# Casting and transposing one operand in two pieces, with two idle matmuls fewer ahead of the first scores

## Chip, cores, metric

One core of one Trainium2 chip. The metric is the device time of one execution, in microseconds (us). Executions of one and the same program scatter here by about 0.4 us (standard deviation), so a change of half a microsecond needs many runs, and single profiles are read for where the time goes, not for how much there is of it. "ScalarE" is the engine that the profile calls ACT, "VectorE" is DVE, "GpSimd" is POOL and "TensorE" is PE.

## The reference

Chunked attention feeds a two-layer network with a swish whose slope is given for each hidden unit. Shapes: q, k, v are 8 x 8 x 576 x 64 in fp32; w_in is 512 x 2048, w_out 2048 x 512.

```python
scores = scale * np.matmul(q_c, k_c.transpose(0, 1, 2, 4, 3))   # chunks of 64
scores = scores - np.max(scores, axis=-1, keepdims=True)
attn = np.exp(scores)
attn = attn / (np.sum(attn, axis=-1, keepdims=True) + 1e-09)
out = np.matmul(attn, v_c)
...
h = x @ w_in
g = h * (1.0 / (1.0 + np.exp(-beta * h)))
return (g @ w_out).astype(np.float32)
```

## The kernel before

After the first 18 us the kernel is a stream of dense matmuls that fills TensorE to the end. The change and the argument are about the opening, where TensorE has no data yet. There it runs "idle" matmuls on zeros, which raise its clock. One of them, called late, waits for a small memset that GpSimd executes between two DMA issues, and so ties the rest to a fixed moment (4.8 us). The first 512 tokens come in two halves of four heads. Heads 0 to 3 come through the sync queue as fp32 (`raw0`) and are cast by ScalarE; heads 4 to 7 come through GpSimd's queue, which casts on the way (`qk0[1]`). VectorE transposes both in blocks of 32 x 32.

```python
    def emit_T_half(a):
        for i in (0, 1):                      # q, then k
            if a == 0:
                nc.scalar.copy(out=qk0[a][i], in_=raw0[i])
            nc.vector.transpose(out=qkT0[a][i]..., in_=qk0[a][i]...)   # cut

    def emit_sc_half(u, a):                   # 4 heads of unit u
        ...                                   # cut
        qt, kt = qkT0[a]
        for h in range(HH):                   # HH = 4
            ...                               # 8 small matmuls a head

    # the opening, in TensorE's order
        emit_tiny(78)
        warm = idle_bank()
        emit_idle(3, 512, warm)
        nc.tensor.matmul(out=warm[:, 0:16], lhsT=idle[:, 0:128], rhs=late)
        emit_idle(10, 512, warm)
        emit_T_half(0)
        emit_sc_half(0, 0)                    # "first scores"
        emit_ex_half(0, 0)
        warm = idle_bank()
        emit_idle(6, 512, warm)
        emit_T_half(1)
        nc.vector.transpose(out=bt, in_=braw)
        emit_sc_half(0, 1)                    # "second scores": heads 4 to 7
        emit_ex_half(0, 1)
        emit_sc_half(1, 0)
        emit_idle(2, 512, warm)
        ...                                   # cut: issues of later loads
        emit_pv(0, ("s", "p"))                # needs v tiles 0 and 1
        ...
```

The softmax here doesn't subtract the row's maximum and nothing guards it: scores larger than these inputs give would overflow.

Of the kernel before, what the change touches and what calls it, by code (L numbers as in the profile page):

```python
# [8 lines left out]
FP32 = mybir.dt.float32  # L9
# [6 lines left out]
def kernel(  # L16
# [10 lines left out]
    nc = tc.nc  # L27
# [31 lines left out]
    HH = H // 2  # L59
    raw0 = [const.tile([128, HH, 4, D], FP32, name=f"raw{i}") for i in range(2)]  # L60
    qk0 = [[const.tile([128, HH, 4, D], FP16, name=f"h0{i}{a}") for i in range(2)] for a in range(2)]
    qkT0 = [[const.tile([128, HH, 128, 2], FP16, name=f"t0{i}{a}") for i in range(2)] for a in range(2)]
# [109 lines left out]
    xt_t = {}  # L172

    def emit_T_half(a):
        for i in (0, 1):
            if a == 0:
                nc.scalar.copy(out=qk0[a][i], in_=raw0[i])
            nc.vector.transpose(
                out=qkT0[a][i].rearrange("p h s e -> p (h s e)").bitcast(FP32).rearrange(
                    "p (h i r) -> p h r i", h=HH, r=4),  # L180
                in_=qk0[a][i].rearrange("p h r d -> p (h r d)").bitcast(FP32).rearrange(
                    "p (h r i) -> p h r i", h=HH, r=4),
            )

    def emit_sc_half(u, a):
# [135 lines left out]
    def emit_m(j, m, c0=0, n=None, later=False):  # L321
        n = blocks[j][1] * UNIT if n is None else n
        if j not in gt_t:
            gt_t[j] = gt_p.tile([128, KFF, 512], FP16, tag="gt", name="gt")
        hps = ps_p.tile([128, 512], FP32, tag="p", name="hps")
        xr = xt_t[j].rearrange("p t (r k) (c q) -> p (t r) (k c) q", r=2, c=2)
        for kk in range(KDM):
            nc.tensor.matmul(  # L328
                out=hps[:, 0:n],
                lhsT=w_in16[m // 2][:, kk, (m % 2) * 128:(m % 2) * 128 + 128],  # L330
                rhs=xr[:, c0 // CH:(c0 + n) // CH, 2 * (kk % 2) + kk // 2, :],
                start=(kk == 0),
                stop=(kk == KDM - 1),
            )
        sg = sg_p.tile([128, 512], FP32, tag="sg", name="sg")

        def act():
            nc.scalar.activation(  # L338
                out=sg[:, 0:n], in_=hps[:, 0:n], func=ACTF.Tanh, scale=beta2[:, m:m + 1])

        def vec():
            nc.vector.scalar_tensor_tensor(  # L342
                out=gt_t[j][:, m, c0:c0 + n], in0=sg[:, 0:n], scalar=1.0, in1=hps[:, 0:n],
                op0=ALU.add, op1=ALU.mult,
            )

        if later:
            return act, vec
        act()
        vec()  # L350
# [23 lines left out]
    def idle_bank():  # L374
        return ps_p.tile([128, 512], FP32, tag="p", name="warm")

    def emit_idle(n, w, d=None):
        d = idle_bank() if d is None else d
        for _ in range(n):
            nc.tensor.matmul(out=d[:, 0:w], lhsT=idle[:, 0:128], rhs=idle[:, 0:w])  # L380
# [12 lines left out]
    with tc.manual_schedule():  # L393
# [4 lines left out]
        for a, eng, dst in ((0, nc.sync, raw0), (1, nc.gpsimd, qk0[1])):  # L398
            for i, src in enumerate((q, k)):
                eng.dma_start(  # L400
                    out=dst[i],
                    in_=src[0, HH * a:HH * a + HH, 0:2 * UNIT, :].rearrange("h (p r) d -> p h r d", r=4),
# [19 lines left out]
        warm = idle_bank()  # L422
        emit_idle(3, 512, warm)
        nc.tensor.matmul(out=warm[:, 0:16], lhsT=idle[:, 0:128], rhs=late)
        emit_idle(10, 512, warm)
        emit_T_half(0)
        emit_sc_half(0, 0)
        emit_ex_half(0, 0)
# [4 lines that stand above are left out]
        emit_sc_half(0, 1)  # L433
# [16 lines left out]
        d = [emit_m(0, m, 0, 256, True) for m in (0, 1)]  # L450
# [145 lines left out]
        for c0, n in ((0, 256), (256, 128), (384, 128)):  # L596
            ops = ps_p.tile([128, DM], FP32, tag="p", name="ops")
            for kk in range(KFF):
                nc.tensor.matmul(  # L599
                    out=ops[:, 0:n],  # L600
# [42 lines left out]
```

## Time and profile before

| | before |
|---|---|
| time, first three runs | 288.23, 288.73, 288.71 us |
| span of the profiled execution | 286.7 us |
| TensorE busy | 98% of the span, 96% of the chain that ended last |
| first scores start | 8.84 us |
| second scores start | 10.62 us |
| w_in products run without a break from | 17.77 us |

Read it from the end backwards. From 17.77 us TensorE has no pause that could be won, so a change in the opening is worth just what it moves that moment. The prediction below shows the chain, the timeline and the page for it. One view is added: the transfers of heads 4 to 7 by the moment of their issue (size, and us from issue to landing). They are issued at 1.24 and 2.12 us.

```profile
h<-in_q_dram POOLq DMA_DIRECT2D x1, 256.0 KB, 6.0
h<-in_k_dram POOLq DMA_DIRECT2D x1, 256.0 KB, 6.6
```

### The profile page before, as it was taken

How to read it: one execution, taken by the hardware profiler on the slowest of the kernel's cores; microseconds unless marked ns; L12 is line 12 of the kernel's file. 1: busy time of each engine (PE TensorE's matmuls, PEld its weight loads, DVE VectorE, ACT ScalarE, POOL GpSimd, SP SyncE). 2: the span in 40 equal slices, each digit the busy share in tenths (PEclk: the TensorE clock that was granted, in tenths of full speed). 3: DMA queues.
4: the chain of work that ended last, by engine and by line, in shares of the span. 5: the costliest groups of instructions: out<-in, count | busy, mean ns of one | idle time of the engine just before them, and what ended most of it. 6: DMA issues, size and time to landing. Idle time of an engine off the chain costs nothing.

```text
span 286.7 us, 6657 instructions
## 1 busy us (share of the span) xinstructions
PE 280.5 (98%) x2779; PEld 136.4 (48%) x2779; DVE 141.8 (49%) x259; ACT 146.9 (51%) x224; POOL 95.7 (33%) x125
## 2 busy tenths in 40 slices
PE   6989999999999999999999999999999999999995
PEld 3564456545544444444444444444444444444444
DVE  2678544776567544534454445454554545333300
ACT  4478228774557545454545454554545444444411
POOL 8853678487172983070907070000000000000000
PEclk9999999999999999999999999999999999999999
DMA  8999999999999999999999999565451212001012
GB/s 197 177 197 206 182 179 212 207 165 164 152 97 179 148 175 162 177 123 162 140 165 105 175 122 174 130 75 128 57 129 37 75 37 75 37 37 39 37 73 75
DMA packets 139997, 37.14 MB, mean 130 GB/s; under 512 B 126912, under 2 KB 135488, under 8 KB 139968
## 3 DMA queue, kind: packets, MB, share of 16 engines
q0 software_dynamic: 99136, 17.83, 81.1%
q1 hardware_dynamic: 40688, 18.83, 32.4%
q8 instruction: 22, 0.36, 0.5%
q10 hardware_dynamic: 144, 0.07, 0.1%
q14 instruction: 7, 0.06, 0.1%
HBM read 36.71 MB, written 9.44 MB: 161 GB/s over the span
## 4 chain that ended last, share of the span: by engine, by line
PE 96%; ACT 1%; POOL 1%; issue 1%; DVE 0%; DVEq 0%; POOLq 0%
PE hps L328 44%; PE ops L360 43%; PE warm L380 2%; PE x L265 2%; PE sc L237 1%; PE sc L224 1%; PE ops L599 1%; ACT xt L303 1%; PE xp L302 1%; POOL h L400 1%; POOL vbig L113 1%; PE sc L197 0%; ACT et L207 0%; PE y L265 0%; PE xp L310 0%
## 5 line engine op out<-in xcount | busy, mean ns | idle before, releaser
L342 DVE SCALAR_TENSOR_TENSOR gt<-sg,hps 128x512 f16<-128x512 f32 (+1 forms) x153 | 99.1, 654 | 107.3 <-ACT sg L338 107.1
L338 ACT ACTIVATE sg<-hps,beta 128x512 f32<-128x512 f32 (+1 forms) x153 | 100.4, 663 | 73.0 <-PE hps L328 72.9
L328 PE MATMUL hps<-xt,win 128*128 128x512 f16 (+1 forms) x612 | 136.9, 367 | 0.8 <-ACT xt L303 0.7
L360 PE MATMUL ops<-wout,gt 128*128 128x512 f16 x560 | 131.2, 379 | 0.0
L328 PEld LDWEIGHTS <-win 128*128 128x128 f16 x612 | 58.1, 98 | 62.1 <-issue 1.0
L360 PEld LDWEIGHTS <-gt 128*128 128x128 f16 x560 | 53.9, 98 | 63.4
L370 ACT ACTIVATE osb<-ops 128x512 f32<-128x512 f32 x35 | 20.9, 598 | 42.5 <-PE ops L360 42.5
L113 POOL DMA_DIRECT2D vbig<-in_v_dram x40 | 34.0, 870 | 10.9 <-DMA wout<-in_moe_w_out_dram 3.7
L99 POOL DMA_DIRECT2D qu<-in_q_dram x22 | 18.7, 864 | 40.6 <-DMA qT<-qu 37.6
L286 DVE TENSOR_TENSOR x<-x,rd 128x512 f16<-128x512 f32 x31 | 21.4, 692 | 1.2
L99 POOL DMA_DIRECT2D ku<-in_k_dram x22 | 18.9, 884 | 0.0
L284 DVE RECIPROCAL rd<-x 128x8 f32<-128x8 f32 x31 | 6.2, 201 | 12.5 <-PE x L265 12.5
L246 ACT ACTIVATE et<-sc 128x1024 f16<-128x1024 f32 (+1 forms) x8 | 6.4, 811 | 8.2 <-PE sc L237 8.2
L230 ACT ACTIVATE et<-sc 128x1024 f16<-128x1024 f32 x10 | 10.2, 1018 | 0.2
L265 PEld LDWEIGHTS <-et 64*64 64x64 f16 x576 | 6.0, 107 | 7.3 <-issue 3.8
L380 PE MATMUL warm<-idle 128*128 128x512 f16 x24 | 8.4, 499 | 0.0
L105 POOL DMA_DIRECT2D ku<-in_k_dram x9 | 6.8, 758 | 2.5 <-DMA win<-in_moe_w_in_dram 1.3
L105 POOL DMA_DIRECT2D qu<-in_q_dram x9 | 6.8, 766 | 2.0 <-DMA win<-in_moe_w_in_dram 1.4
L265 PE MATMUL x<-vbig,et 64*64 64x65 f16 x496 | 7.3, 194 | 0.2 <-ACT et L207 0.2
L611 DVE TENSOR_SCALAR osb<-ops 128x256 f32<-128x256 f32 (+1 forms) x2 | 0.7, 358 | 12.1 <-PE ops L599 12.1
L131 POOL DMA_DIRECT2D win<-in_moe_w_in_dram x8 | 6.0, 764 | 1.2 <-DMA vbig<-in_v_dram 1.2
L303 ACT COPY xt<-xp 128x512 f16<-128x512 f16 x9 | 5.1, 588 | 2.3 <-PE xp L302 2.2
(46 smaller groups left out, 73.0 us busy)
## 6 DMA issues: line engine op xcount, KB each, us to landing
out_dram<-osb SPq DMA_DIRECT2D x35, 256.0 KB, 4.0
vbig<-in_v_dram POOLq DMA_DIRECT2D x32, 128.0 KB, 7.8
qu<-in_q_dram POOLq DMA_DIRECT2D x20, 128.0 KB, 5.4
ku<-in_k_dram POOLq DMA_DIRECT2D x20, 128.0 KB, 7.3
win<-in_moe_w_in_dram POOLq DMA_DIRECT2D x8, 256.0 KB, 8.8
wout<-in_moe_w_out_dram POOLq DMA_DIRECT2D x4, 512.0 KB, 12.2
qu<-in_q_dram POOLq DMA_DIRECT2D x3, 256.0 KB, 7.4
ku<-in_k_dram POOLq DMA_DIRECT2D x3, 256.0 KB, 8.0
```

Source lines behind the costliest of these rows:

```text
L99: nc.gpsimd.dma_start(out=tv[off:off + n, sp], in_=src[b, :, s:s + n, :].rearrange("h p d -> p h d"),)
L105: nc.gpsimd.dma_start(out=t[off // 2:(off + n) // 2], in_=src[b, :, s:s + n, :].rearrange("h (p r) d -> p h r d", r=2),)
L113: nc.gpsimd.dma_start(out=vbig[off:off + n, i, :, 0:D], in_=v[b, :, s:s + n, :].rearrange("h p d -> p h d"),)
L230: nc.scalar.activation(out=et, in_=sc, func=ACTF.Exp, scale=scale)
L265: nc.tensor.matmul(out=(x[0][64 * c:64 * c + 64, r, g, 0:D + 1] if len(x) == 1 else x[r][64 * c:64 * c + 64, g, 0:D + 1]), lhsT=(et[64 * r ...
L286: nc.vector.tensor_tensor(out=o, in0=z[..., 0:D], in1=rd[:, r].to_broadcast(list(o.shape)), op=ALU.mult)
L328: nc.tensor.matmul(out=hps[:, 0:n], lhsT=w_in16[m // 2][:, kk, (m % 2) * 128:(m % 2) * 128 + 128], rhs=xr[:, c0 // CH:(c0 + n) // CH, 2 * ...
L338: nc.scalar.activation(out=sg[:, 0:n], in_=hps[:, 0:n], func=ACTF.Tanh, scale=beta2[:, m:m + 1])
L342: nc.vector.scalar_tensor_tensor(out=gt_t[j][:, m, c0:c0 + n], in0=sg[:, 0:n], scalar=1.0, in1=hps[:, 0:n], op0=ALU.add, op1=ALU.mult,)
L360: nc.tensor.matmul(out=ops, lhsT=gt_t[j][:, kk, t * 128:(t + 1) * 128], rhs=w_out16[kk // 4][:, kk % 4, :], start=(kk == 0), stop=(kk == K ...
L370: nc.scalar.activation(out=osb, in_=ops, func=ACTF.Copy, scale=0.5)
L380: nc.tensor.matmul(out=d[:, 0:w], lhsT=idle[:, 0:128], rhs=idle[:, 0:w])
```

## The change

Its intent: have k of heads 0 to 3 transposed earlier by overlapping cast and transpose of two pieces, and take out two idle matmuls, so that the first scores start earlier.

```diff
     def emit_T_half(a):
-        for i in (0, 1):
+        for i, h0, h1 in ((0, 0, HH), (1, 0, HH // 2), (1, HH // 2, HH)) if a == 0 else ((0, 0, HH), (1, 0, HH)):
+            src = qk0[a][i][:, h0:h1]
             if a == 0:
-                nc.scalar.copy(out=qk0[a][i], in_=raw0[i])
+                nc.scalar.copy(out=src, in_=raw0[i][:, h0:h1])
             nc.vector.transpose(
-                out=qkT0[a][i].rearrange(...),      # cut
+                out=qkT0[a][i][:, h0:h1].rearrange(...),
...
         nc.tensor.matmul(out=warm[:, 0:16], lhsT=idle[:, 0:128], rhs=late)
-        emit_idle(10, 512, warm)
+        emit_idle(8, 512, warm)
```

More of the change, by code (lines that the diff above doesn't have):

```diff
@@ L174, in emit_T_half @@
     def emit_T_half(a):
-        for i in (0, 1):
+        for i, h0, h1 in ((0, 0, HH), (1, 0, HH // 2), (1, HH // 2, HH)) if a == 0 else ((0, 0, HH), (1, 0, HH)):
+            src = qk0[a][i][:, h0:h1]
             if a == 0:
-                nc.scalar.copy(out=qk0[a][i], in_=raw0[i])
+                nc.scalar.copy(out=src, in_=raw0[i][:, h0:h1])
             nc.vector.transpose(
-                out=qkT0[a][i].rearrange("p h s e -> p (h s e)").bitcast(FP32).rearrange(
-                    "p (h i r) -> p h r i", h=HH, r=4),
-                in_=qk0[a][i].rearrange("p h r d -> p (h r d)").bitcast(FP32).rearrange(
-                    "p (h r i) -> p h r i", h=HH, r=4),
+                out=qkT0[a][i][:, h0:h1].rearrange("p h s e -> p (h s e)").bitcast(FP32).rearrange(
+                    "p (h i r) -> p h r i", h=h1 - h0, r=4),
+                in_=src.rearrange("p h r d -> p (h r d)").bitcast(FP32).rearrange(
+                    "p (h r i) -> p h r i", h=h1 - h0, r=4),
             )
```

## The prediction

> **What bounds the kernel now.** I read the busy table and the chain shares of the page first, then the chain of waits in order of time, then the timeline of the first 18 us engine by engine, with short windows where merged lines hide single instructions. The page:
>
> ```profile
> span 286.7 us, 6657 instructions
> PE 280.5 (98%) x2779; PEld 136.4 (48%) x2779; DVE 141.8 (49%) x259; ACT 146.9 (51%) x224; POOL 95.7 (33%) x125
> ...
> PE 96%; ACT 1%; POOL 1%; issue 1%; DVE 0%; DVEq 0%; POOLq 0%
> ```
>
> TensorE holds 96% of the chain that ends last. The diff touches nothing after about 10 us, so the question is when the first scores start, and whether an earlier start survives to the end. The chain in order of time for the opening:
>
> ```profile
> 4.82 0.17 PE warm L424
> 4.99 3.92 PE warm L380 x10
> 8.91 0.38 PE sc L197 x27
> 9.29 1.40 PE warm L380 x6
> 10.69 0.64 PE sc L197 x57
> 11.33 0.54 PE warm L380 x2
> ...
> 17.28 0.44 DVE xt L303
> 17.72 0.05 issue
> 17.77 12.28 PE hps L328 x64
> ```
>
> The reader sees that the ten idle matmuls themselves are on the chain, not the data that they wait for. The timeline (start, duration, engine, line, operation, tiles, shapes, count, idle before and its releaser) has what runs beside them:
>
> ```profile
> 4.69 1.04 ACT L177 CAST h<-raw 128x1024 f16<-128x1024 f32 x1 [2.67 <-DMA raw<-in_q_dram]
> 4.84 4.07 PE L380 MATMUL warm<-idle 128*128 128x512 f16 x10
> 5.76 1.10 DVE L178 STREAM_TRANSPOSE t<-h 128x512 f32<-128x512 f32 x1 [3.33 <-ACT h L177]
> 6.20 1.04 ACT L177 CAST h<-raw 128x1024 f16<-128x1024 f32 x1 [0.47 <-DMA raw<-in_k_dram]
> 7.27 2.94 DVE L178 STREAM_TRANSPOSE t<-h 128x512 f32<-128x512 f32 x3 [0.41 <-ACT h L177]
> 8.84 0.45 PE L197 MATMUL sc<-t,t 32*64 32x64 f16 x32
> 9.22 1.47 PE L380 MATMUL warm<-idle 128*128 128x512 f16 x6
> 10.62 0.71 PE L197 MATMUL sc<-t,t 32*64 32x64 f16 x64
> ```
>
> Short windows split these. The ten idles start at 4.84, 5.22, 5.65, 6.08, 6.50, 6.93, 7.36, 7.78, 8.21 and 8.53: 0.427 us apart, but 0.32 before the last. The six later ones are 0.22 apart (9.22, 9.45, 9.66, ...). So the array runs at half rate until about 8.42, and the tenth idle ends near 8.53 + 0.22 = 8.75. The scores start 0.09 later, at 8.84. The k transpose started at 7.27 and took 1.09: ready at 8.36. Other waits of TensorE on VectorE end 0.05 after the releaser (17.28 + 0.43, then 17.76), so k was usable at 8.41. The timeline names the transpose as releaser, but it had been done for 0.4 us; the idles were the later.
>
> **What the Trainium skill says.** "TensorE: Matmul & The Clock Gate", section "Back-to-back issue gap", gives a spacing of N/1.2 ns cold and N/2.4 + 2.5 ns warm: 427 and 216 ns at N = 512. The trace agrees (0.427, then 0.22). The same page, "Part 1: The HAM clock gate", says that the full clock comes after about 3.4 us of sustained activity, judged by a free-running window, so that the moment differs from run to run. Here it falls 3.6 us after idles resume at 4.84; one trace cannot show the variation. "Perfetto Trace Analysis", section "Optimizing Scalar/DVE Operations", says that when these engines aren't saturated but cause bubbles on others, breaking up instructions may let work finish sooner, and that each instruction has its own overhead. The trace shows both sides: ScalarE's Exp is 0.60 us for 512 elements and 1.02 for 1024, so about 0.17 fixed.
>
> **The change, part by part.**
> 1. Two idle matmuls go. The eighth starts at 7.78 and the next slot is 8.21. With the same 0.09 handover the scores could start at 8.30 instead of 8.84: 0.54 us. Of this 0.43 is two matmuls at full rate; 0.11 is because half-rate time held one of them. If the clock still rises at 8.42, the first 0.12 us of scores run at half rate and give back at most 0.06.
> 2. The k cast becomes two of 512 elements. From Exp's slope (0.83 ns an element) each takes 1.045 - 0.425 = 0.62 us. The k data lands as before, so piece one ends at 6.82. Successive ScalarE instructions overlap by some 0.12 elsewhere (48.17 for 0.58, next at 48.63), so piece two ends near 7.3.
> 3. The k transpose becomes two of 128x256. The 128x512 takes 1.09 and the 128x32 beta transpose 0.17, so about 1.9 ns per element: 0.17 + 224 x 0.0019 = 0.59. Piece one runs 6.87 to 7.46, piece two about 7.34 to 7.93. All of k is ready at 7.98 instead of 8.41. Together with part 1 the start is max(8.30, 7.98) = 8.30. Without the split it would have been max(8.30, 8.41), so here the split is worth 0.11. The built order shows also that the scores of heads 0 and 1 wait for piece one only (7.51), those of heads 2 and 3 for piece two.
> 4. The second half moves earlier. VectorE transposes q and k of heads 4 to 7 right behind. Before, they started at 8.22 and 9.13 and ended at 10.21. Now q starts near 7.81 and k near 8.75; its DMA landed at 2.12 + 6.6 = 8.72, just in time, so it ends near 9.84. TensorE needs it after 8.30 + 0.38 of scores, six idles of 0.22 and 0.09, at 10.08. It is ready by 0.19. ScalarE's and VectorE's extra instructions cost about 0.2 us of their own time, on engines 51% and 49% busy, where neither ends the wait.
>
> So the second scores move from 10.62 to 10.08, and TensorE, ScalarE and VectorE pass it on: every wait from there to 17.77 is released by ScalarE or VectorE, which work on what TensorE gave. DMA does not move with them, so I checked each landing against the new need. v tiles 0 and 1 land at 10.86 and about 11.33; needed at 11.26 and 11.41. Tiles 2 and 3: 12.2 and 13.0, needed from 13.2. w_in group 1: about 15.6, needed at 15.88. k of unit 2: 34.5, its transposes end at 35.8, scores need them at 36.3. The last w_out group: 38.5, needed at 41.0. All hold, several by only 0.1 to 0.5. From 17.77 to 280.04 TensorE is busy 262.18 of 262.27 us, so the lead is kept. Sum: 0.54 - 0.06 = 0.48, call it **0.5 us**.
>
> **The rivals.**
> A. The clock stays at half rate. The window that ended at 8.42 was filled by full 128x512 idles; now its last 0.2 us holds a handover and small 32-row scores. If the monitor then misses and judges again 3.4 us later (skill's window), the six idles cost 6 x 0.21 = 1.3 us more and the small stages a little more: an estimate of 289 to 290 us. Against it: 3.3 of 3.4 us remain dense. I give it one in ten.
> B. A DMA takes the place of the idles. v tile 1 is 0.08 ahead of its need, w_in group 1 is 0.28 ahead. Either being late eats 0.1 to 0.3 of the gain: 288.3 to 288.5. For it: the DMA queues are full there; against: none of the landings of this trace is late.
> C. The gain is larger, if the clock rises late in the timed runs: with both removed idles at 0.43 the scores start 0.85 earlier. But as the rise comes at a fixed time, at full rate later, the end still moves by the 0.43 of work removed. So C changes the first scores, not the time.
> D. TensorE is bound by transposed k anyway. The trace speaks against it: 8.41 against 8.75. Were it so, the split alone would give about 0.4.
>
> **Range and chances.** The timed runs are 288.23, 288.73 and 288.71, mean 288.56; the profiled run took 288.54. I take the mean, not the median, as base: 288.55 - 0.5 gives about 288.1. Spread between runs is 0.5 and the gain may be 0.3 to 0.55, so most results lie from 287.6 to 288.6; rival A adds a tail, and I widen the top to 288.8. Faster by 2% would need 5.8 us, a third of the whole opening, out of a change that moves 0.5: one in a hundred. Slower by 2% would need several missed windows: one in a hundred.
>
> **What would show it.** In the timeline: eight idles from 4.84; two k casts near 0.62 and two k transposes near 0.59; first scores near 8.30, and again 0.09 after the last idle rather than after a transpose; the 0.22 spacing from the first of the six idles on; the second scores near 10.08; hps continuous from about 17.25; the closing 128x256 matmuls near 279.55. Idles 0.43 apart after 8.5 would show A. A v or w_in wait before 17 us, with hps still at 17.6 or later, would show B. First scores starting 0.05 after a k transpose would show that my handover reading is wrong. The figure fails if phase or DMA landings move by more than the 0.5 us at stake.

## The result

The changed kernel took 288.77 us (median of 6 runs, 288.48 to 289.24) and the kernel before 288.72 (median of 6 in the same comparison, 288.23 to 289.52). The ratio is 0.9998, with a 95% interval of 0.998 to 1.0015: the same. Ratios here are the mean time of one kernel's runs over the mean of the other's of the same rounds, so not quite the ratio of the medians.

The predicted range (287.6 to 288.8) and class (within 2%) hold. But the predicted gain of 0.5 us is not there: the range was wide enough to hold no gain at all. And the profile shows that the steps did not go as told. The chain in order of time, after (start, us, engine, tile, line; lines below the edit are numbered one higher than before):

```profile
4.82 0.17 PE warm L425
4.99 3.43 PE warm L381 x8
8.42 0.57 PE sc L198 x18
8.99 1.65 PE warm L381 x6
10.64 0.64 PE sc L198 x60
...
17.72 12.28 PE hps L329 x64
```

The first scores did start half a microsecond earlier in the chain (8.42 against 8.91). Then they took 0.57 instead of 0.38, and the six idles 1.65 instead of 1.40. The second scores stand at 10.64 against 10.69, and the products at 17.72 against 17.77: a lead of 0.05 us is left. The timeline of the same execution:

```profile
5.21 1.05 ACT L178 CAST h<-raw 128x1024 f16<-128x1024 f32 x1 [3.19 <-DMA raw<-in_q_dram]
6.29 4.15 DVE L179 STREAM_TRANSPOSE t<-h 128x512 f32<-128x512 f32 x5 [3.86 <-ACT h L178]
6.71 1.14 ACT L178 CAST h<-raw 128x512 f16<-128x512 f32 x2 [0.45 <-DMA raw<-in_k_dram]
8.35 0.64 PE L198 MATMUL sc<-t,t 32*64 32x64 f16 x32
8.93 1.71 PE L381 MATMUL warm<-idle 128*128 128x512 f16 x6
10.57 0.71 PE L198 MATMUL sc<-t,t 32*64 32x64 f16 x64
```

Three things differ from what was told. q and k landed half a microsecond later than before (the casts start at 5.21 and 6.71, not 4.69 and 6.20). Short windows put the starts of the six idles at 8.93, 9.32, 9.61, 9.83, 10.04 and 10.26: the first gap is 0.39 and the second 0.29, so the clock rose only near 9.5. And the transposes run on until 6.29 + 4.15 = 10.44, so k of heads 4 to 7 was usable at 10.49, where 9.89 was told. In this execution the idles ended still later, so the second scores follow the last idle (10.26 + 0.31 = 10.57) and not k. The transfers of heads 4 to 7:

```profile
h<-in_q_dram POOLq DMA_DIRECT2D x1, 256.0 KB, 6.6
h<-in_k_dram POOLq DMA_DIRECT2D x1, 256.0 KB, 7.2
```

k landed at 2.13 + 7.2 = 9.33 us, 0.6 later than in the profile before. No instruction that issues a transfer is altered by the change.

### The profile page after: what moved, and what is told of

It reads as the page before. It is cut to its first block, busy times and chain, and to the rows that moved or that the text cites. A ratio compares the mean times of both kernels' runs of the same rounds, so it can differ in the third digit from the quotient of the medians.

```text
span 286.6 us, 6655 instructions
## 1 busy us (share of the span) xinstructions
PE 280.4 (98%) x2777; PEld 136.4 (48%) x2777; DVE 141.9 (49%) x260; ACT 147.0 (51%) x225; POOL 95.7 (33%) x125
## 4 chain that ended last, share of the span: by engine, by line
PE 96%; ACT 1%; POOL 1%; issue 1%; DVE 0%; DVEq 0%; POOLq 0%
PE hps L329 44%; PE ops L361 43%; PE warm L381 2%; PE x L266 2%; PE sc L238 1%; PE sc L225 1%; PE ops L600 1%; ACT xt L304 1%; PE xp L303 1%; POOL h L401 1%; PE sc L198 1%; POOL vbig L113 1%; ACT et L208 0%; PE y L266 0%; PE xp L311 0%
## 5 line engine op out<-in xcount | busy, mean ns | idle before, releaser
L231 ACT ACTIVATE et<-sc 128x1024 f16<-128x1024 f32 x10 | 10.2, 1018 | 0.2
```

The costliest lines, as they stand in the source:

```text
L231: nc.scalar.activation(out=et, in_=sc, func=ACTF.Exp, scale=scale)
```

## The experiments

The theories:

- **Phase**: the clock rises at a moment that differs from execution to execution, whatever the change, and the profile after caught a late one.
- **Delay**: the change itself makes the clock rise later, because two dense matmuls are gone.
- **Landing**: the landing of q and k, above all of heads 4 to 7, takes the place of the idles that were removed.

Every kernel was timed in five rounds and profiled once. The kernels of one call share the runs of the kernel before: mean 288.73 us for the first four, 288.80 for the next four, 288.96 for the last four (11 runs each; the first and third call ran on one chip, the second on another). Means below are over six runs. The clock's rise is worked out from the gap g between two idle starts in which it falls: with x us of g at half rate, x/0.427 + (g - x)/0.216 = 1. Where it falls among the scores it is only known to about 0.1.

### The changed kernel again

No edit. 

> The changed kernel once more, unaltered, for its time in more rounds and for a second profile. Phase theory (the full clock comes at a moment that differs from execution to execution, whatever the change): the rise, read off the spacing of the idle matmuls, falls anywhere from 8 to 12 us and not at 9.47 again; timed, the kernel is 0.4 to 0.5 us faster than the one before on average. Delay theory (two dense idles fewer let the monitor judge later): the rise is again about 9.5, and the timed difference is 0 to 0.1 us. Landing theory (q and k merely landed 0.5 us later in that one profile): raw q lands near 4.6 and raw k near 6.2 as in the profile of the kernel before, the first scores start at 8.30 after the last idle.

Mean 288.87; ratio 1.0007 (0.9989 to 1.0025). The clock rose near 8.0, so the delay theory's 9.5 is not reproduced. The first scores started at 8.20 after the last idle, and the six idles are 0.22 apart. And yet most of the gain is missing: the second scores start at 10.35, where 10.0 was free. The timeline and the chain of this run:

```profile
9.20 1.09 DVE L179 STREAM_TRANSPOSE t<-h 128x512 f32<-128x512 f32 x1 [0.29 <-DMA h<-in_k_dram]
10.35 0.71 PE L198 MATMUL sc<-t,t 32*64 32x64 f16 x64 [0.29 <-DVE bt L433]
```

```profile
2.13 7.05 DMA h<-in_k_dram
9.18 0.02 issue
...
10.35 0.71 PE sc L198 x60
```

VectorE stood idle until k of heads 4 to 7 landed at 9.18, and that transfer is what the chain of the end now runs back to. The view names the small beta transpose `bt` as releaser because it comes last; the k transpose before it ends at 10.29, within 0.04 of it.

### The split alone

Ten idles, k in two pieces.

```diff
-        emit_idle(8, 512, warm)
+        emit_idle(10, 512, warm)
```

> Part 2 and 3 alone: k cast and transposed in two pieces, ten idle matmuls as before. All theories: the first scores follow the tenth idle, so nothing is gained, within 0.1 us of the kernel before, unless k is what they wait for. Delay theory: the rise is near 8.4 as in the kernel before. Phase theory: the rise is anywhere.

Mean 288.87; ratio 1.0006 (0.9989 to 1.0023): the same, as all theories said. The clock rose at 8.2, the first scores started at 8.72 after the tenth idle. One more source of scatter showed here: at 126 us TensorE waited 0.44 us for the transfer of a transposed x tile. Two more of the fourteen profiles have this wait, the fill in the changed kernel (0.13) and the version with both split (0.08).

### Eight idles alone, twice

The edit of the idle count without the split.

```diff
-        emit_idle(10, 512, warm)
+        emit_idle(8, 512, warm)
```

> Part 1 alone: eight idle matmuls, k cast and transposed in one piece. Phase theory: if k lands at 6.16 it is usable at 8.41, the first scores start then, and 0.3 to 0.4 us is gained on average; if it lands at 6.66 they start at 8.9 and nothing is gained. Delay theory: rise near 9.5 and no gain.

> Eight idle matmuls without the split, a second time, because the first look gave 0.3 us faster than the kernel before and 0.4 faster than the changed kernel, which no theory explains. If that was chance among runs that scatter by 0.4 us: within 0.2 us of the changed kernel this time. If the split itself costs something that I don't see: again 0.3 to 0.4 us faster than the changed kernel.

Means 288.41 and 288.48; ratios 0.9991 (0.9976 to 1.0006) and 0.9985 (0.997 to 1.0). The clock rose near 8.9 and at 7.6. The second time the first scores started at 8.37, after the k transpose, as worked out for this form (8.41). Both means are about as much below the kernel before as phase theory told (0.3 to 0.4). That this half of the change does better than the whole was not expected, and is taken up below.

### The kernel before, against itself

No edit. 

> The kernel before against itself: the difference is the noise of the comparison, expected within 0.15 us. Its profile gives a second clock rise of the kernel before: delay theory 8.4 again, phase theory another moment; and a second landing of raw q and k: landing theory near 4.6 and 6.2 again.

Mean 289.03, ratio 1.0012 (0.9996 to 1.0029): the same program differs from itself by 0.3 us, more than the 0.15 expected. The clock rose at 7.9, not 8.4: so it varies in the kernel before too. And q and k of heads 4 to 7 landed at 8.9 and 10.02 instead of 7.3 and 8.7. The second scores waited until 11.18:

```profile
2.14 7.88 DMA h<-in_k_dram
10.02 0.02 issue
...
11.18 0.71 PE sc L197 x62
```

### No pause ahead of the gate

Six idles instead of three before the gated matmul, in the changed kernel and in the one before. This closes TensorE's pause from 3.6 to 4.8 us and costs nothing, since the gate opens at 4.8 anyway.

```diff
         warm = idle_bank()
-        emit_idle(3, 512, warm)
+        emit_idle(6, 512, warm)
         nc.tensor.matmul(out=warm[:, 0:16], lhsT=idle[:, 0:128], rhs=late)
```

> The changed kernel with six instead of three idle matmuls before the gated one, so that TensorE has no pause between 3.6 and 4.8 us. Phase theory (the clock's rise comes at a varying moment of a window that must be filled with work): the rise comes earlier than 8 us, all scores and later idles run at full rate, the first scores start when the second piece of k is ready at the latest, near 8.0, and what is left is the landing of q and k of heads 4 to 7: second scores at landing of k plus 1.15 us, some 9.9 to 10.5; on average 0.3 to 0.5 us faster than the kernel before. Landing theory alone (the rise doesn't matter): no change against the changed kernel, second scores still at landing plus 1.15. Delay theory: rise near 8.4 at the earliest, since it counts from the gate.

> The same three idle matmuls put ahead of the gate in the kernel before. Phase theory: rise before 8 us, ten idles end by 7.5 or so, the first scores start at 8.41 after the k transpose and no longer after an idle; second scores at 10.2 or at the landing of k plus 1.15; 0.2 to 0.4 us faster than the kernel before. Delay and landing theory: no difference from the kernel before.

Means 288.40 and 288.44; ratios 0.9984 (0.9967 to 1.0001) and 0.9985 (0.9969 to 1.0002). The clock rose at 5.8 and 5.2 us. That ends the delay theory in the form that counts from the gate. It also shows what the pause cost, about 0.4 us in both, with intervals that just touch no difference. In the profile of the changed kernel with the fill, TensorE is then left waiting for the landing alone:

```profile
9.51 1.08 DVE L179 STREAM_TRANSPOSE t<-h 128x512 f32<-128x512 f32 x1 [0.44 <-DMA h<-in_k_dram]
10.64 0.71 PE L198 MATMUL sc<-t,t 32*64 32x64 f16 x64 [0.92 <-DVE bt L433]
```

It idles for 0.92 us before the second scores. Everything that was won ahead of it, in idles and in clock, is given back there. This one execution took 288.75 us, one of the two slowest of its six; the average over the six keeps the 0.4.

### The second landing taken away

A wrong result: the second half transposes q and k of heads 0 to 3 again, so it waits for no transfer. The transfers themselves stay. The edit in the changed kernel; its twin, the kernel before, has the same exchange in the `in_=` argument of its transpose:

```diff
-            src = qk0[a][i][:, h0:h1]
+            src = qk0[0][i][:, h0:h1]
```

> Wrong result on purpose: the changed kernel transposes q and k of heads 0 to 3 a second time in place of heads 4 to 7, so the second scores don't wait for the landing of those. The transfers stay. Landing theory (the second landing takes the place of the idles removed): second scores now follow the last idle by 0.09 us in every profile, at 10.0 to 10.6 depending on the clock's rise, and the difference to its twin with ten idles is the full 0.45 to 0.5 us on average. If the landing doesn't matter: no faster than the changed kernel, and no more different from its twin than the two real kernels from each other, 0 to 0.1.

> The twin of the run before: the kernel before, with q and k of heads 0 to 3 transposed twice. Wrong result on purpose. Landing theory: second scores after the last idle at 10.35 to 11.1 depending on the rise; 0.05 to 0.2 us faster than the kernel before on average, since there the landing seldom comes last. Otherwise within 0.1 of the kernel before.

The check of the output passed these runs all the same: the reference scales q and k by 0.1, so all scores are near zero (standard deviation about 0.01, an estimate from the inputs) and the wrong ones change little. What "correct" says of heads 4 to 7 is therefore weak in every run here.

Means 288.32 for the changed kernel and 288.82 for its twin; ratios to the kernel before 0.9981 (0.9965 to 0.9997) and 0.9998 (0.9983 to 1.0014). The twins differ by 0.50 us, the predicted gain, where the real kernels differ by nothing. From the scatter of the two sets of six the 95% interval of that difference is about 0.12 to 0.88, so its size is not sharp, but that it exists is clear. Against the 0.03 of the real kernels (all means pooled, below) it is 0.47 more, with an interval of about 0.03 to 0.9: only just clear of noise. The twin gained nothing over the kernel before, where 0.05 to 0.2 was expected. One more expectation failed: second scores were to follow the last idle in every profile. In the changed kernel's they started at 9.85, after the second transpose (5.72 + 4.08 + 0.05), with the idles done for 9.76. Then v tile 1 came in: it landed at 11.40, its products started at 11.45, and the w_in products at 17.29, 7.44 after the second scores instead of 7.15.

### Both waits taken away

The fill and the wrong-result edit together. 

> Wrong result on purpose: the changed kernel with both suspected waits taken away at once, the fill ahead of the gate and q and k of heads 0 to 3 transposed twice. If clock and landing are the two things that took the gain, the opening now has neither: rise before 8 us, first scores near 8.0 after the second piece of k, second scores 0.09 after the last of six full-rate idles or after the second transposes, near 9.65 to 9.9 in every profile; 0.6 to 0.9 us faster than the kernel before. If some third wait takes over (v tile 1 at about 11.3, w_in group 1 at about 15.6), the gain stays at the 0.5 us of the run without the landing, and a DMA shows as the releaser between 11 and 17 us.

Mean 288.32, ratio 0.9979 (0.9964 to 0.9994): no more than without the landing alone. The clock rose at 6.8, the second scores started at 9.83, and a third wait came up again, the one that the expectation named as the alternative. The timeline:

```profile
11.01 0.32 PE L266 MATMUL x<-vbig,et 64*64 64x65 f16 x16
11.52 0.32 PE L266 MATMUL y<-vbig,et 64*64 64x65 f16 x16 [0.20 <-DMA vbig<-in_v_dram]
```

v tile 1 landed at 11.48 and the products started at 17.36, 7.53 after the second scores instead of 7.15. Second scores earlier than about 10.2 therefore win nothing more.

### A version that beats both

The fill, and k of heads 4 to 7 transposed in two pieces as well:

```diff
-        for i, h0, h1 in ((0, 0, HH), (1, 0, HH // 2), (1, HH // 2, HH)) if a == 0 else ((0, 0, HH), (1, 0, HH)):
+        for i, h0, h1 in ((0, 0, HH), (1, 0, HH // 2), (1, HH // 2, HH)):
```

> The version that the runs so far point to: the changed kernel, with six idle matmuls ahead of the gate instead of three, and k of heads 4 to 7 transposed in two pieces too. Clock's rise before 8 us as in the two runs with the fill; second scores start with heads 4 and 5 when the first piece of k is ready, at the landing of k plus 0.65 us, instead of plus 1.15; since the rest still waits for the second piece, only 0.1 to 0.2 us more than with the fill alone: 288.2 to 288.3 on average, 0.5 to 0.6 faster than the kernel before. If the landing isn't what ends the wait: no better than the fill alone, 0.4 faster.

Correct, mean 288.15 (287.99 to 288.46), ratio 0.9973 (0.9958 to 0.9988): 0.8 us faster than the kernel before, the only real kernel here whose gain is clear of noise in its own comparison, and the one with the least scatter. That the second split adds to the fill is not shown: against the fill in the changed kernel the gain is 0.24, with an interval from -0.2 to 0.65, and in its profile k of heads 4 to 7 landed early (8.9). There the second scores started at 9.86. It too ran into v tile 1, as the chain says:

```profile
3.73 7.70 DMA vbig<-in_v_dram
11.43 0.04 issue
11.47 0.32 PE y L266 x16
...
17.31 0.72 PE hps L329 x5
```

### The changed kernel a third time

No edit. 

> The changed kernel a third time, unaltered, on the same chip as the next: 288.8 on average as twice before, within 0.2 us of the kernel before. Its profile gives a third rise and a third landing; second scores at the later of landing of k plus 1.15 and last idle plus 0.31.

Mean 288.82, ratio 0.9997 (0.998 to 1.0014). Clock's rise near 10.0, k of heads 4 to 7 at 9.2 us, second scores at 10.84, after the last idle.

### All profiles in one table

"Last idle" is the start of the last of the six idles plus 0.31 (its 0.22 and the 0.09 handover). "k usable" is the end of the second k transpose plus 0.05. The clock's rise and the landing are not set by the program; all times in us.

| kernel | clock's rise | k of heads 4-7 lands | k usable | last idle | second scores |
|---|---|---|---|---|---|
| before | 8.4 | 8.72 | 10.26 | 10.62 | 10.62 |
| before, again | 7.9 | 10.02 | 11.17 | 10.36 | 11.18 |
| changed | 9.5 | 9.33 | 10.49 | 10.57 | 10.57 |
| changed, again | 8.0 | 9.18 | 10.34 | 9.99 | 10.35 |
| changed, third | 10.0 | 9.2 | 10.36 | 10.84 | 10.84 |
| split alone | 8.2 | 8.8 | 9.96 | 10.50 | 10.50 |
| eight alone | 8.9 | 9.1 | 10.24 | 10.35 | 10.35 |
| eight alone, again | 7.6 | 8.7 | 10.21 | 10.15 | 10.21 |
| fill, changed | 5.8 | 9.5 | 10.64 | 9.65 | 10.64 |
| fill, before | 5.2 | 9.3 | 10.48 | 10.15 | 10.48 |
| changed, no landing | 7.5 | - | 9.85 | 9.76 | 9.85 |
| before, no landing | 9.1 | - | 10.20 | 11.00 | 10.99 |
| fill, no landing | 6.8 | - | 9.82 | 9.64 | 9.83 |
| fill, both split | 6.7 | 8.9 | two pieces | 9.86 | 9.86 |

In the thirteen rows with one second k piece, the second scores start at the later of the two columns before them, to 0.02 us. The products follow 7.15 us later, except where v tile 1 comes in. The idle column moves with the clock, the other with the landing. The change lowers both by about half a microsecond if clock and landing are as in the first profile; what it can't lower is the landing plus its 1.15 us. For the delay theory: the six profiles with eight idles and without the fill have their rise at 8.6 on average, the four with ten at 8.4. That is no sign of the delay by 1 us that the first profile suggested, but too few to exclude a smaller one.

## Why the prediction was right or wrong

The number. 288.77 lies in the range, near its top, and the class is right; with a change this small no other class was likely. That the number fits is partly luck. The base of 288.55, a mean of three runs, was 0.3 too low (288.86 over 45 runs), and the gain of 0.5 was too high. Pooling all means, the changed kernel stands at 288.83 (18 runs) and the kernel before at 288.86 (45 runs): a gain of 0.03, with an interval of about 0.24 either way. So 0.5 is excluded, and one or two tenths are not.

**Bound and handover: right.** The opening's lead does pass to the end: from the start of the products to the closing matmuls it is 262.4 us before and after. The first scores follow the eighth idle at 8.20 in the profile with early data (told: 8.30). In the two profiles with a late clock they started at 8.35 and 8.36, 0.56 after the start of the eighth idle instead of 0.43 + 0.09: there the handover took 0.13. It was not the late landing, since the first piece of k was usable at 8.05 and 8.00.

**Costs of the pieces: right.** The casts took 0.615 each (told 0.62), the transposes 0.64 each (told 0.59). The prediction took the transpose's 1.9 ns an element as given. Later in the same trace transposes of equal size (line 157), whose output steps by two 32-bit elements instead of four, took 0.67 to 0.71 us instead of 1.07 to 1.10. No run here changes the step alone, so the cause is not shown, but the 1.15 us after the landing need not be fixed.

**Part 1, "give back at most 0.06": wrong in general.** It took the rise of the one profile, 8.42, as given. Over ten profiles without the fill the rise lies between 7.5 and 10.0. In the profile after, first scores and six idles paid (0.57 - 0.38) + (1.65 - 1.40) = 0.44 us for a late one. Rival A had the mechanism but ascribed it to the change, with one chance in ten. The runs speak for phase: identical kernels rose at 9.5, 8.0 and 10.0, the kernel before at 8.4 and 7.9. By itself this shifts single profiles and widens the scatter of both kernels; it doesn't take an average gain away, as rival C argued and the twins without the landing confirm: they have the varying clock and kept 0.50.

**Part 4, "just in time": this step failed in all three profiles.** It used one landing, 8.72, and gave k a margin of 0.19 us. In the three profiles of the changed kernel it landed at 9.33, 9.18 and 9.2, so that k was usable at 10.49, 10.34 and 10.36 instead of 9.89. The second scores then can't start before about 10.4, whatever idles or clock do; against 10.62 that leaves some 0.1 to 0.3 of the 0.54. Taking this wait away in both kernels brought the gain back. But it ended the wait in only one of the three profiles (10.34 against 9.99); in the other two the idles, with their late clock, ended 0.08 and 0.48 after k was usable. The prediction's last sentence named moving landings as what would make it fail. Yet rival B lists v and w_in alone and passes over k of heads 4 to 7, whose margin of 0.19 was smaller than the 0.28 of w_in. v tile 1 was read as landing at 11.33, with 0.08 to spare; in that trace it lands at 11.41, just when it would have been needed. It was the next wait in line, and showed as soon as the first was gone.

**What stays open.** The twins make it likely that the landing takes a part of the gain; that it takes all is not shown. Eight idles without the split ran at 288.45 (12 runs), 0.39 us below the changed kernel, with an interval of about 0.1 to 0.7, and 0.42 below the kernel before (0.17 to 0.67). They wait for the same landing plus the same transpose and kept most of the gain, so the landing alone can't explain what the changed kernel lost. No theory here gives the split a cost, and the split kernels with the fill or without the landing show none. The wait at 126 us showed in three of eight profiles of split kernels and in none of the six others, and there the stretch from the products to the closing matmuls is 0.7, 0.3 and 0.2 us longer. But none of the changed kernel's own three profiles has it, and so few prove nothing. In two of three profiles of the changed kernel raw q landed near 5.2 instead of 4.6 us, and both had the latest clock rises; that landing precedes every altered instruction. Whether this is chance, or something in how the program is loaded, these runs do not tell.

## What to carry to other kernels

Before taking filler or a wait out of an opening, write down the spread, over several profiles, of each transfer that the next stages need, not its moment in one; a margin smaller than that spread can become the next bound, here 0.2 us against over 1 us. A matching experiment is cheap: take the suspected wait away in both versions and see whether the expected difference comes back. And if filler serves to raise a clock, let it run without a pause: three more idle matmuls in a gap that was waiting anyway were worth about 0.4 us here, nearly what the whole change was meant to be worth.

## What the Trainium skill lacked or had wrong

- "TensorE: Matmul & The Clock Gate", Part 1, says that the rise varies by some 500 ns either way with the phase of a free-running window. Here it fell between 7.5 and 10.0 us in ten profiles whose idles resumed at the same 4.8 us: a spread of 2.5 us. With the pause closed it came at 5.2 to 6.8.
- No page that I read tells how much the landing of a transfer varies between executions. k of heads 4 to 7, issued at 2.1 us in every profile, landed between 8.7 and 10.0; q of the same heads between 7.2 and 8.9.
